# Loading w4 in five pieces of 11, 9, 5, 2 and 1 rows instead of eight

## Chip, cores, metric

One core of one Trainium2 chip. The metric is the device time of one execution in microseconds. Ratios of times come with a 95% interval; "same" means within 2%. Besides the time there is the profile: the span of one execution (about 1.8 us shorter than the time) and the trace of every instruction, DMA packet and semaphore event in it. In the lines shown from it, PE is TensorE, DVE VectorE, ACT ScalarE and SP the sync engine; a "q" behind the name means the engine's instruction sequencer, and L191 is line 191 of the kernel. A load is counted in 16 completion counts, one from each DMA engine; it has arrived with the last of them.

## The reference

One decoded token goes through two branches whose results are added. Branch A is attention over a cache of 65536 keys (32 query heads, 4 key/value heads of width 128). Branch B is a small mixer and a two-layer MLP:

```python
h2 = _gelu(_layernorm(x1, axis=-1) @ w3) @ w4      # w4: 3584 x 1024, bf16
...
return x + _A_ref(xn, A_k_cache, A_v_cache, A_wq, A_wo) + _B_ref(xn, ...)
```

Every weight and the whole cache are read once, 169.87 MB. There is little arithmetic per byte.

## The kernel before

All large operands pass through three buffers of 8 MB, in a fixed order: wq, w3, w1 and w2, then K and V of eight units, wo between the last K and the last V, and w4 at the end. A load is issued when a buffer comes free. All of them go through the sync engine's one DMA queue, so they run in order.

w4 is laid out as 128 partitions x 28 rows; a "row" here is 1024 bf16 elements (2 KB) in each partition, 256 KB in all. It is loaded in pieces, so that its matmuls can start before all of it is there:

```python
W4_PIECES = (6, 5, 6, 4, 3, 2, 1, 1)
...
            elif it == "w4":
                w4_v = B_w4.rearrange("(m c) n -> m c n", c=FC)
                c0 = 0
                for n in W4_PIECES:
                    go(out=t[:, c0 * D:(c0 + n) * D], in_=w4_v[:, c0:c0 + n, :].rearrange("p c n -> p (c n)"))
                    c0 += n
```

At the end, TensorE adds everything into one PSUM bank (`row_acc`), two matmuls for each row of w4. `early` is the number of rows, 11, that come before the last group's projection:

```python
    add_projection()
    compute_v(NU - 1)
    early = sum(W4_PIECES[:2])
    compute_w4(0, early)
    project(HKV - 1)
    compute_w4(early, FC)

    out_t = ogpool.tile([64, 512], BF16, name="out_t", tag="og")
    nc.scalar.copy(out=out_t[:], in_=psB[0:64, :])
    nc.scalar.dma_start(out=out[0, 0, :].rearrange("(j n) -> j n", j=2), ...)
```

One thing is not in this source. The framework gives each DMA one of eight completion semaphores, in rotation, and at the end it makes the sync engine wait for all of them.

## Time and profile before

| | before |
|---|---|
| time, median of 4 runs | 402.25 us (402.11 to 402.31) |
| span of the profiled run | 400.3 us |
| DMA engines busy | 98.6% of the span (main queue) |
| last V arrives | 379.32 us |
| last of w4 arrives | 396.73 us |
| from there to the end | 3.60 us |

The page's head and some of its lines. The digits are tenths of busy time in 40 equal slices of the span; the line "q1" gives packets, MB and busy share of the sync engine's queue.

```profile
span 400.3 us, 2563 instructions
PE 236.0 (59%) x1348; PEld 45.2 (11%) x854; DVE 208.9 (52%) x154; ACT 27.3 (7%) x35; POOL 5.3 (1%) x28
...
DMA  9998999999999999999999999999999998999895
...
q1 hardware_dynamic: 4560, 169.87, 98.6%
```

No compute engine is near full, and the DMA engines are busy nearly everywhere. I read the kernel as bound by its loads.

The chain of waits, its last pieces (start in us, length, what):

```profile
379.33 17.39 DMA big<-in_B_w_dram
396.73 0.04 issue
396.77 0.40 PE psB L191 x2
397.17 0.02 issue
397.19 0.58 ACT out_t L455
```

From the arrival of the last V, w4 streams alone for 17.4 us. After its last byte come two matmuls, the cast and the store.

TensorE in the same stretch (start, length, line, what, count; in brackets its idle time before and what ended it):

```profile
386.21 2.30 PE L191 MATMUL psB<-big,hT 128*1 128x512 bf16 x10
388.44 0.80 PE L403 MATMUL pm_e<-ol,sel8big 128*128 128x129 f32 x2
389.17 1.50 PE L191 MATMUL psB<-big,hT 128*1 128x512 bf16 x12
390.51 1.89 PE L191 MATMUL psB<-big,oT 128*1 128x512 bf16 x16
392.23 2.97 PE L191 MATMUL psB<-big,hT 128*1 128x512 bf16 x26
395.47 1.03 PE L191 MATMUL psB<-big,hT 128*1 128x512 bf16 x6 [0.27 <-DMA big<-in_B_w_dram]
396.77 0.38 PE L191 MATMUL psB<-big,hT 128*1 128x512 bf16 x2 [0.27 <-DMA big<-in_B_w_dram]
```

The matmuls over `hT` are w4's, those over `oT` the last projection. TensorE catches up with the stream and twice waits for it, 0.27 us each. The last two matmuls start 0.04 us after the last arrival.

The sync engine's waits, the lines about w4's issue (L153) and the program's end (L482): total us, times, longest.

```profile
SPq L482 <- DMA big<-in_B_w_dram: 17.0, 3, 15.8
...
SPq L153 <- DMA big<-in_A_v_cache_dram: 14.5, 1, 14.5
...
SPq L482 <- DMA out_dram<-out_t: 2.7, 1, 2.7
```

The last two pieces reuse semaphores of wo and of the last V, and so the last piece could not be issued before the last V had landed. (A further line, 0.6 us for `PEq`, is the meeting of the engines at the very end; it is left out here.)

### The profile page before, as it was taken

The numbers are of one execution on the slowest core, as the hardware profiler recorded it, in microseconds if no ns is written. First come the engines' busy times: TensorE is split into PE (matmuls) and PEld (weight loads), VectorE is DVE, ScalarE is ACT, GpSimd is POOL, SyncE is SP. The second block draws the span as 40 slices with busy tenths as digits, with TensorE's granted clock in tenths as the row PEclk, the third lists the DMA queues.
The fourth block names the chain that finished last, engine by engine and source line by source line (L and its number), as shares of the span: only waits on it lengthen the run. The fifth ranks groups of instructions, "written<-read, shape, count | busy, mean of one in ns | idle before, by whom it ended". The sixth has DMA issues, their size and how long they took to land.

```text
span 400.3 us, 2563 instructions
## 1 busy us (share of the span) xinstructions
PE 236.0 (59%) x1348; PEld 45.2 (11%) x854; DVE 208.9 (52%) x154; ACT 27.3 (7%) x35; POOL 5.3 (1%) x28
## 2 busy tenths in 40 slices
PE   0561960591678247922965195629453946594986
PEld 0210000010200110011102010201020102000222
DVE  1601010965196549644953994279349931975040
ACT  1001010003000200020002000100100020002000
POOL 2000000000000000000000000000000000000000
PEclk9995795597669666978796789568865986697989
DMA  9998999999999999999999999999999998999895
GB/s 419 419 453 371 435 471 458 426 419 419 421 426 465 452 426 414 426 426 432 445 460 426 419 426 419 447 439 452 426 421 426 432 445 385 432 481 426 385 417 201
DMA packets 4575, 170.01 MB, mean 425 GB/s; under 512 B 467, under 2 KB 469, under 8 KB 982
## 3 DMA queue, kind: packets, MB, share of 16 engines
q1 hardware_dynamic: 4560, 169.87, 98.6%
q8 instruction: 8, 0.13, 0.1%
q14 instruction: 1, 0.01, 0.0%
q10 hardware_dynamic: 6, 0.00, 0.0%
HBM read 169.87 MB, written 0.00 MB: 424 GB/s over the span
## 4 chain that ended last, share of the span: by engine, by line
DMA 51%; DVE 26%; PE 16%; ACT 3%; another core or an unknown queue 2%; issue 1%; DVEq 0%; ACTq 0%
DMA big<-in_A_k_cache_dram 31%; DVE big L327 19%; DMA big<-in_A_v_cache_dram 10%; PE sc L332 8%; PE oacc L382 6%; DMA big<-in_A_wq_dram 6%; DMA big<-in_B_w_dram 4%; DVE p_sb L353 3%; DVE mx L337 3%; ACT p_sb L350 3%; PE psq L257 2%; DVE m L341 0%; PE pm_mx L339 0%; PE pm_mx L346 0%
## 5 line engine op out<-in xcount | busy, mean ns | idle before, releaser
L332 PE MATMUL sc<-big,qdiag 128*128 128x512 bf16 x512 | 129.5, 414 | 62.7 <-DVE big L327 57.2
L327 DVE STREAM_TRANSPOSE big<-big 128x4096 f32<-128x4096 f32 x32 | 139.4, 4413 | 49.4 <-DMA big<-in_A_k_cache_dram 49.4
L382 PE MATMUL oacc<-big,p_sb 128*32 128x512 bf16 x512 | 46.9, 539 | 34.5 <-DVE p_sb L353 34.5
L337 DVE TENSOR_REDUCE mx<-sc 128x1 f32<-128x2048 f32 x8 | 18.3, 2291 | 30.0 <-PE sc L332 30.0
L332 PEld LDWEIGHTS <-qdiag 128*128 128x128 bf16 x128 | 13.2, 103 | 174.7 <-issue 145.9
L350 ACT ACTIVATE p_sb<-sc,nball 128x2048 bf16<-128x2048 f32 x8 | 15.7, 1967 | 217.8 <-DVE nball L348 217.8
L353 DVE STREAM_TRANSPOSE p_sb<-p_sb 128x2048 bf16<-128x2048 bf16 x8 | 18.5, 2311 | 18.0 <-ACT p_sb L350 18.0
L382 PEld LDWEIGHTS <-p_sb 128*32 128x32 bf16 x512 | 17.1, 129 | 61.0 <-DVE p_sb L353 35.1
L257 PE MATMUL psh<-big,ln_rep_b 128*32 128x512 bf16 (+1 forms) x64 | 12.4, 941 | 7.6 <-DMA big<-in_B_w_dram 7.6
L421 PE MATMUL o_acc<-big,oT 128*1 128x512 bf16 x48 | 12.8, 437 | 2.4 <-ACT p_sb L350 2.4
L339 PE MATMUL pm_mx<-ident_f,mx 128*1 128x128 f32 x8 | 2.2, 273 | 19.1 <-DVE mx L337 19.1
L296 DVE STREAM_TRANSPOSE h_row<-h_row 128x896 bf16<-128x896 bf16 x1 | 1.1, 1111 | 20.8 <-ACT h_row L295 20.8
L391 DVE SCALAR_TENSOR_TENSOR og<-oacc,wb,og 128x512 f32<-128x512 f32 x4 | 3.0, 746 | 16.7 <-PE oacc L382 16.7
L191 PE MATMUL psB<-big,hT 128*1 128x512 bf16 x56 | 8.1, 424 | 0.6 <-DMA big<-in_B_w_dram 0.5
L427 DVE COPY o_rows<-o_acc 1x1024 f32<-1x1024 f32 x1 | 1.2, 1211 | 13.6 <-PE oacc L382 13.6
L205 PE MATMUL pm_ln<-ln_rowsum_a,ones_f 128*128 128x1 f32 x2 | 0.6, 348 | 12.5 <-DVE ln_rowsum_a L203 12.5
L403 PE MATMUL pm_e<-ol,sel8big 128*128 128x129 f32 x8 | 2.8, 446 | 7.9 <-DVE ol L402 7.9
L257 PE MATMUL psq<-big,ln_rep_a 128*32 128x512 bf16 x64 | 6.2, 573 | 1.5 <-DMA big<-in_A_wq_dram 1.5
L281 POOL COPY qdiag<-qx 32x32 bf16<-32x32 bf16 x16 | 3.2, 203 | 279.5 <-PE sc L332 249.6
L196 DVE STREAM_TRANSPOSE x_t<-x_row 32x256 bf16<-32x256 bf16 x4 | 2.5, 616 | 8.1 <-DMA x_row<-in_A_x_dram 8.0
L269 DVE CAST q_row<-psq 128x512 bf16<-128x512 f32 x1 | 0.7, 691 | 8.4 <-PE psq L257 8.4
L346 PE MATMUL pm_mx<-ident_f,rep 1*128 1x1 f32 x8 | 1.8, 223 | 5.0 <-DVE rep L343 5.0
(95 smaller groups left out, 73.2 us busy)
## 6 DMA issues: line engine op xcount, KB each, us to landing
big<-in_A_wo_dram SPq DMA_DIRECT2D x1, 8192.0 KB, 36.0
big<-in_B_w_dram SPq DMA_DIRECT2D x1, 7168.0 KB, 38.3
big<-in_B_w_dram SPq DMA_DIRECT2D x2, 2048.0 KB, 46.3
big<-in_B_w_dram SPq DMA_DIRECT2D x2, 1536.0 KB, 27.3
big<-in_B_w_dram SPq DMA_DIRECT2D x1, 1280.0 KB, 24.1
big<-in_B_w_dram SPq DMA_DIRECT2D x1, 1024.0 KB
big<-in_B_w_dram SPq DMA_DIRECT2D x1, 768.0 KB, 30.7
big<-in_B_w_dram SPq DMA_DIRECT2D x1, 512.0 KB, 31.5
```

The costliest lines, as they stand in the source:

```text
L191: nc.tensor.matmul(psB[32 * j:32 * j + lhsT.shape[1], :], lhsT=lhsT, rhs=rhs, start=start, stop=False, tile_position=(0, 32 * j), skip_gro ...
L257: nc.tensor.matmul(acc[32 * q:32 * q + 32, i, 0:n], lhsT=rep[:, c, :], rhs=cols(c, i, q), start=(c == 0), stop=(c == DC - 1), tile_positio ...
L281: nc.gpsimd.tensor_copy(out=qdiag[at, LEAD:].rearrange("p (x c) -> p x c", x=4)[:, :, 32 * a:32 * a + 8], in_=qx[at, :, 8 * g:8 * g + 8])
L327: nc.vector.transpose(out=words, in_=words)
L332: nc.tensor.matmul(sc[:, e, :], lhsT=qdiag[:, c0:c0 + P], rhs=cols[:, s, e, :, b2, :, r], start=(s == 0 and b2 == 0 and r == 0), stop=(s = ...
L337: nc.vector.reduce_max(out=mx[:], in_=sc[:].rearrange("p e n -> p (e n)"), axis=AX.X)
L350: nc.scalar.activation(out=p_sb[:], in_=sc[:], func=ACTF.Exp, bias=nball[:, b:b + 1], scale=SCALE, accum_out=group["lall"][:, b:b + 1])
L353: nc.vector.transpose(out=flat, in_=flat)
L382: nc.tensor.matmul(oacc[32 * q:32 * (q + 1), :], lhsT=pT[:, e, 32 * t:32 * (t + 1)], rhs=vt[:, :, e, t, :], start=(e == 0 and t < 4), stop ...
L391: nc.vector.scalar_tensor_tensor(out=og[:], in0=oacc[:], scalar=wb[:, 1:2], in1=og[:], op0=ALU.mult, op1=ALU.add)
L403: nc.tensor.matmul(pe[:, 0:DH + 1], lhsT=sel8big[:], rhs=ol[:], start=True, stop=True)
L421: nc.tensor.matmul(tail["rows"][0:1, h2, :], lhsT=oT[g][:, j:j + 1], rhs=wt[:, g, j, 512 * h2:512 * (h2 + 1)], start=(g == 0 and j == 0), ...
```

## The change

The intent: fewer and larger transfers in a stretch bound by the DMA engines, with the last piece still one row, so that little work is left behind the last arrival. The first piece covers the same 11 rows as the first two did.

```diff
-W4_PIECES = (6, 5, 6, 4, 3, 2, 1, 1)
+W4_PIECES = (11, 9, 5, 2, 1)
...
-    early = sum(W4_PIECES[:2])
+    early = W4_PIECES[0]
```

## The prediction

> What bounds the kernel now. In the page's slices the 16 DMA engines are 98 to 99% busy almost from end to end, at about 425 GB/s; 169.87 MB have to be read. TensorE is busy 59% of the span, VectorE 52%. The chain of waits ends plainly: V of the last unit lands at 379.33 us, then "DMA big<-in_B_w_dram" takes 17.39 us to 396.73, then two matmuls of 0.40, a ScalarE cast of 0.58, the store, end at 400.3. So w4 streams alone for 17.4 us, and the rest of the work there hides under it.
>
> What the change does. Same 7.34 MB, same slot, same release (first w4 issue at 361.64, 17.7 us before its bytes move). Eight transfers become five. The last piece stays one row, so what follows the last landing is unchanged. Two waits of the sync engine go: the last two pieces reuse the completion semaphores of wo and of the last V (14.5 us in the wait view; last issue only at 379.3). I count this as worth nothing: that piece was still queued 17 us before it landed.
>
> What a transfer costs. The completion counts in the trace put the last arrival of the eight pieces (6, 5, 6, 4, 3, 2, 1, 1 rows) at 383.02, 386.09, 389.80, 392.29, 394.17, 395.43, 396.08 and 396.73. The steps fit 0.61 us per row plus 0.04 per piece. Three pieces fewer: 0.12 us. A second estimate from packet records: medians of 84 ns for 2048 B, 312 for 8192, 613 for 16384, 2420 for 65536 give about 8.6 ns per packet beside the bytes, and a completion takes 9; 24 data packets and 3 completions fewer per engine make 0.23 us. I take 0.12 to 0.23. The Trainium skill, "DMA: Bandwidth & Descriptors", section "Why small descriptors are slow (HBM only)", names a fixed overhead per packet; the trace agrees, at most 8.6 ns here. The same page, "Anatomy of one DMA", fits a fixed 2.0 us per transfer (on another issue path). Three times that would be 6 us; I reject it: the transfers queue back to back, and windows from 380 to 394 us show the engines 99 to 103% busy across four boundaries between pieces.
>
> Does TensorE lose? The first 11 rows had landed by 386.09, and the w4 matmuls started only at 386.21, after the projection rows; the wait for 11 rows costs 0.1 us at most. After the last group's projection, at 392.2, 18 matmuls of the 9-row piece run to 394.3 (0.114 us each, as the 26 there before). I estimate landings at 386.07, 391.6, 394.65, 395.9 and 396.55. Ten matmuls fit between the third and fourth, four between the fourth and fifth (0.5 to 0.6 us: tight). TensorE should still be waiting for the last row.
>
> On the critical path: all of the 0.12 to 0.23 us, as the w4 stream ends the chain. Predicted 402.1 us, range 401.7 to 402.5 (three runs before spread 0.2). Chances: faster by over 2% 0.005, within 2% 0.99, slower 0.005.
>
> Right if: 4128 packets on the sync queue instead of 4560; last w4 landing 17.15 to 17.3 us after V's; two matmuls behind it, after a short wait; five issues in a few us, no wait for V.
>
> Wrong if: a completion costs the stream more than this; the spread between engines (2.0 us from first to last arrival of a piece) changes; or TensorE, kept waiting by coarser pieces, has matmuls left when the last row lands.

## More of the kernel before

The three waits under L482 are the closing ones: first for w4, and only then, for 2.7 us, for the store.

## The result

402.16 us (402.09 to 402.19, 4 runs) against 402.25 (402.11 to 402.31). The ratio is 0.9998, interval 0.9981 to 1.0015: the same. (A ratio is the mean of one kernel's fast runs over the mean of the other's in the same rounds, so it is not quite the ratio of the medians.) Two later batches of five runs gave 402.14 against 402.05 and 402.12 against 402.14. No gain can be seen in the time.

The page after:

```profile
span 400.4 us, 2560 instructions
PE 229.6 (57%) x1348; PEld 44.3 (11%) x854; DVE 209.0 (52%) x154; ACT 27.3 (7%) x35; POOL 5.4 (1%) x28
...
DMA  9998999999999999999999999999999999999994
...
q1 hardware_dynamic: 4128, 169.87, 98.5%
```

432 packets fewer for the same bytes, as predicted. The chain after, its last pieces:

```profile
363.49 33.11 DMA big<-in_B_w_dram
396.60 0.04 issue
396.65 0.40 PE psB L191 x2
397.05 0.02 issue
397.07 0.58 ACT out_t L455
```

The DMA piece is longer only because nothing now ties the last piece's issue to the last V; the chain goes back to its issue at 363. The last row arrives at 396.604 with the last V at 379.408: the stretch is 17.20 us, where it was 17.41 (396.728 less 379.319). The arrivals of V are taken from the semaphore events of the trace, as are those in the tables below. The stream did gain 0.21 us.

But the span did not get shorter. From the last arrival of w4 to the end it is now 3.80 us, where it was 3.60. TensorE, the cast and the issue of the store follow as before (397.07 + 0.58). The sync engine's waits after, the lines that answer to those above (there is none for L153 on V any more):

```profile
SPq L482 <- DMA out_dram<-out_t: 35.4, 1, 35.4
SPq L482 <- PEq L482: 0.6, 2, 0.4
```

The closing waits now begin with the store. The sync engine stands at that wait for 35.4 us, from just after its last issue at 363.5. All the other closing waits come after it, when their loads have long arrived. The trace shows the last completion count of the store at 399.44 us before and 399.32 after, and the end of the span at 400.33 and 400.40. So 0.89 us pass behind the store before, and 1.09 after. That is where the gain seems to have gone. (The last V came 0.09 us later in this profile. Over the 14 profiles it came between 379.20 and 379.50, with no order that I see. Such scatter is as large as the gain, so the arguments below rest on the stretches of the trace and not on the totals.)

TensorE after:

```profile
386.16 1.24 PE L191 MATMUL psB<-big,hT 128*1 128x512 bf16 x9 [0.73 <-DMA big<-in_B_w_dram]
387.32 0.74 PE L403 MATMUL pm_e<-ol,sel8big 128*128 128x129 f32 x2
388.00 3.06 PE L191 MATMUL psB<-big,hT 128*1 128x512 bf16 x13
390.51 2.27 PE L191 MATMUL psB<-big,oT 128*1 128x512 bf16 x16
392.40 4.62 PE L191 MATMUL psB<-big,hT 128*1 128x512 bf16 x34
```

It waits 0.73 us for the first 11 rows, then works almost without a gap to the end. Still its last two matmuls start 0.04 us after the last row's arrival, as before. The coarser pieces used up slack and cost no time.

### The profile page after: what moved, and what is told of

Its sections match the earlier page's. It is cut to its first block, busy times and chain, and to the rows that moved or that the text cites. A ratio compares the mean times of both kernels' runs of the same rounds, so it can differ in the third digit from the quotient of the medians.

```text
span 400.4 us, 2560 instructions
## 1 busy us (share of the span) xinstructions
PE 229.6 (57%) x1348; PEld 44.3 (11%) x854; DVE 209.0 (52%) x154; ACT 27.3 (7%) x35; POOL 5.4 (1%) x28
## 4 chain that ended last, share of the span: by engine, by line
DMA 56%; DVE 24%; PE 14%; ACT 2%; another core or an unknown queue 2%; issue 1%; SPq 0%; DVEq 0%; ACTq 0%
DMA big<-in_A_k_cache_dram 42%; DVE big L327 19%; DMA big<-in_B_w_dram 8%; PE sc L332 8%; DMA big<-in_A_wq_dram 5%; PE oacc L382 4%; DVE p_sb L353 2%; DVE mx L337 2%; ACT p_sb L350 2%; PE psq L257 1%; SPq L153 0%; PE pm_mx L339 0%; DVE m L341 0%; PE pm_mx L346 0%
## 5 line engine op out<-in xcount | busy, mean ns | idle before, releaser
L382 PE MATMUL oacc<-big,p_sb 128*32 128x512 bf16 x512 | 42.2, 502 | 34.5 <-DVE p_sb L353 34.5
L421 PE MATMUL o_acc<-big,oT 128*1 128x512 bf16 x48 | 11.9, 413 | 2.4 <-ACT p_sb L350 2.4
```

The costliest lines, as they stand in the source:

```text
L382: nc.tensor.matmul(oacc[32 * q:32 * (q + 1), :], lhsT=pT[:, e, 32 * t:32 * (t + 1)], rhs=vt[:, :, e, t, :], start=(e == 0 and t < 4), stop ...
L421: nc.tensor.matmul(tail["rows"][0:1, h2, :], lhsT=oT[g][:, j:j + 1], rhs=wt[:, g, j, 512 * h2:512 * (h2 + 1)], start=(g == 0 and j == 0), ...
```

## The experiments

Theory: w4's stretch is bound by the stream; a piece costs its packets and little else; and the saved 0.21 us was given back in the order of the closing waits. Rivals: a transfer has a large cost of its own; nothing changed but noise; the removed wait for V was part of the effect; TensorE, not the stream, holds the end. Twelve runs were made, all with the right result, each timed in five rounds beside the kernel before (for experiment 7 four times are on record). They came in three batches on three chips: experiments 1 to 4, 5 to 8 and 9 to 12; the kernel before had 402.05, 402.24 and 402.14 us in them. The second batch held no run of the changed kernel, so there its stretches are compared with those of the other batches. "Stretch" is the time from the last V's last arrival to w4's last arrival; "close" is from the store's last completion count to the end of the span.

### 1. The changed kernel once more

No edit.

> The changed kernel once more, as the measure for the other three of this batch. My theory: the w4 stretch (last arrival of the last V to last arrival of w4) is 17.2 us again, 0.2 shorter than with eight pieces (17.4), and the total 0.0 to 0.3 us below the kernel before. Rival 'nothing but noise': the stretch is within 0.05 us of 17.4 in this run. Rival 'given back at the end': the stretch is 17.2, but the time from the last w4 arrival to the end of the span is again longer than before (3.8 us against 3.6).

402.14 us against 402.05 before in this batch. Stretch 17.18, close 1.09. Noise is ruled out as the reading of the trace: in three profiles of the changed kernel the stretch is 17.20, 17.18 and 17.21, and the close 1.09 each time. With eight pieces it is 17.41 and, in experiment 11, 17.39.

TensorE took another course in this profile. It ran at its full granted clock from 386.5 to 390 us (1.00, where the profile above had 0.63) and waited three times for pieces, 1.9 us in all. In the third profile (0.56 there) it waited for none long enough to be listed, and the chain view even follows TensorE back instead of the load. In all three the last two matmuls start 0.04 us after the last row's arrival.

### 2. 28 pieces of one row

```diff
-W4_PIECES = (11, 9, 5, 2, 1)
+W4_PIECES = (1,) * 28
...
-    early = W4_PIECES[0]
+    early = 11
```

> 28 pieces of one row, projection still after row 11. Theory: the stretch grows with the pieces. From the fit of arrivals (0.04 us per piece) 23 pieces more than five cost 0.9 us: stretch 18.1 us; from packet records (8.6 ns per packet, 9 per completion: 184 packets and 23 completions more) 1.8 us: stretch 19.0 us. Total 0.7 to 1.6 us above the kernel before. Rival 'a transfer has a large cost of its own, hidden because few were changed': 23 times 0.3 us or more, at least 7 us over. Rival 'the piece count does nothing': under 0.2 us over. The many waits of the sync engine (each issue waits for the piece eight earlier) should cost nothing, since eight pieces in flight are 5 us of stream.

403.93 us, 1.88 over the kernel before, ratio 1.0046 (1.0032 to 1.0059). Stretch 18.74: 1.55 us for 23 more pieces, 0.068 each. This lies in the expected range of the stretch, nearer to the packet estimate. The total is a little over its range. The terms that the range left out are in the trace: the close is 1.08 instead of 0.89, and the last two matmuls took 0.61 us instead of 0.40. The large cost of a transfer (0.3 us or more) is ruled out, and so is no cost at all.

### 3. Five pieces, but packets of one row

```diff
-  go(out=t[:, c0 * D:(c0 + n) * D], in_=w4_v[:, c0:c0 + n, :].rearrange("p c n -> p (c n)"))
+  go(out=t[:, 0:FC * (D + 8)].rearrange("p (c n) -> p c n", c=FC)[:, c0:c0 + n, 0:D], in_=w4_v[:, c0:c0 + n, :])
...
-  row_acc(j, hT[:, c:c + 1], wt[:, D * c + 512 * j:D * c + 512 * (j + 1)])
+  row_acc(j, hT[:, c:c + 1], wt[:, (D + 8) * c + 512 * j:(D + 8) * c + 512 * (j + 1)])
```

> Five pieces as in the changed kernel, but rows laid 1032 elements apart, so that no packet can be longer than 2048 B: as many data packets as with 28 pieces, 23 completions fewer. If what a piece costs is its packets, this run's stretch equals that of the 28 pieces within 0.25 us (18.1 to 19.0 us). If it is the completion (or the transfer as such), the stretch stays near 17.2 to 17.4 us. Matmuls unchanged.

403.73 us, stretch 18.86, close 1.09. The queue lines of the page, first of the 28 pieces:

```profile
q1 hardware_dynamic: 7440, 169.87, 98.6%
```

and of this run:

```profile
q1 hardware_dynamic: 7072, 169.87, 98.7%
```

The difference of 368 packets is 23 completions on 16 engines; the data packets are the same 3584 of 2048 B. With five completions the stretch is as long as with 28 (even 0.12 us longer, which stays unexplained: the padded rows also start at other addresses). So what a piece costs is its packets: (18.86 - 17.18) us over 184 more packets per engine is 9.1 ns per packet, and from 28 pieces, completions included, it is 8.4. The edit changed one thing more: issuing the five pieces took the sync engine 26.9 us, to 388.8. The last issue was still over 9 us ahead of its landing and the DMA engines were full (share 1.04 to 1.05 from 380 to 394 us), so the issue did not hold the stream there.

### 4. Four more rows to read

```diff
                 c0 = 0
+                go(out=t[:, FC * D:(FC + 4) * D], in_=w4_v[:, 0:4, :].rearrange("p c n -> p (c n)"))
                 for n in W4_PIECES:
```

> The changed kernel with four more rows (1 MB) read into unused space ahead of w4. Theory, the w4 stream alone sets the end: 4 x 0.61 + 0.04 = 2.5 us later, total 2.2 to 2.6 us over the changed kernel of this batch. Rival 'the tail is held by TensorE or by the sync engine's waits as much as by the stream': under 1.5 us.

404.39 us, 2.25 over the changed kernel of the batch, as expected; stretch 19.68, 2.50 longer. The stream sets the end almost one for one (the close, 1.02, is 0.07 shorter here, and the last V came 0.27 earlier).

### 5. The last three pieces merged

```diff
-W4_PIECES = (11, 9, 5, 2, 1)
+W4_PIECES = (11, 9, 8)
```

> Pieces 11, 9, 8: the last three of the change merged. Theory: the stream saves 0.1 to 0.15 us, but 16 instead of 2 matmuls stand behind the last arrival; at 0.11 us each (full rate as after the projection) to 0.21 (the slower rate seen at 388 us of the changed kernel) the end comes 1.4 to 2.9 us later than in the changed kernel. Rival 'pieces at the end cost as much as they hide': within 0.3 us of it.

403.37 us, 1.13 over the kernel before in this batch (402.24), ratio 1.0029 (1.0016 to 1.0041). The stretch is 17.08, 0.1 shorter, and the span 1.3 us longer than the changed kernel's. That is just under the expected range. The last pieces of its chain:

```profile
396.49 0.04 issue
396.53 1.91 PE psB L191 x16
398.44 0.02 issue
398.46 0.58 ACT out_t L455
```

16 matmuls took 1.91 us, where two took 0.40. Of these 1.51 us, 0.1 came back in the stream and 0.09 in the close, which is 1.00 here. A short last piece is worth far more than the packets it costs.

### 6. One piece

```diff
-W4_PIECES = (11, 9, 5, 2, 1)
+W4_PIECES = (28,)
...
-    early = W4_PIECES[0]
+    early = 11
```

> w4 in one piece of 28 rows. Theory: last arrival about 0.2 to 0.3 us sooner than with five pieces, then the 56 w4 matmuls and the last projection (16) behind it: 72 x 0.11 to 0.21 us minus the two that stand there anyhow: 7 to 12 us over the changed kernel. Rival 'each transfer costs 2 us as its fixed share': four transfers fewer give 8 us back and the total is about even with the changed kernel.

411.04 us, 8.8 over the kernel before, ratio 1.0228 (1.0214 to 1.0242): slower. The stretch is the shortest of all, 16.92, but 72 matmuls then stand behind it:

```profile
396.37 0.04 issue
396.41 9.67 PE psB L191 x72
```

Four transfers fewer gave 0.26 us back, not 8.

### 7. The first two pieces merged

```diff
-W4_PIECES = (11, 9, 5, 2, 1)
+W4_PIECES = (20, 5, 2, 1)
...
-    early = W4_PIECES[0]
+    early = 11
```

> Pieces 20, 5, 2, 1, projection still after row 11: merges the first two of the change, to see how much slack TensorE has at the front. Theory: its w4 work starts at 391.6 instead of 386.1 us. 40 matmuls of w4, 16 of the projection and the row sums before it (0.8 us) then take at least 6.9 us at 0.114 each, to 398.5, and 16 more for the last three pieces, to 400.3, where the changed kernel is done at 397.0: 2.5 to 4 us over the changed kernel, with the last row long landed. Rival 'TensorE has slack for any first piece': within 0.3 us.

406.74 us, 4.5 over the kernel before, ratio 1.0113 (1.0099 to 1.0127). The last row arrived at 396.49, and nobody waited for it:

```profile
361.67 29.82 DMA big<-in_B_w_dram
391.49 0.04 issue
391.53 10.09 PE psB L191 x72
401.63 0.02 issue
401.65 0.58 ACT out_t L455
```

The direction held, the size was over the range (2.5 to 4 over the changed kernel). I had reckoned with 0.114 us per matmul. The 72 took 0.140 on average. The stretches of the profile, with the granted TensorE clock (PEclk) as third figure from the end:

```profile
391.50:396.00 4.50, 4.47 (x22) 1.40 (x23) 0.00 (x0) 0.00 (x0) 0.00 (x0) 0.51 0.75 305
396.00:402.00 6.00, 5.61 (x52) 2.08 (x48) 0.00 (x0) 0.35 (x1) 0.00 (x0) 1.00 0.00 0
```

In the first stretch, at 0.51, 22 matmuls ran in 4.5 us; in the second, at 1.00, the other 50 in 5.6. So the slack at the front ends somewhere between 11 and 20 rows, and 11 is what the change chose.

### 8. The wait for V put back

```diff
                 for n in W4_PIECES:
+                    if c0 == FC - 1:
+                        for e in range(3):
+                            go(out=t[0:16, FC * D + 512 * e:FC * D + 512 * (e + 1)], in_=w4_v[0:16, 0, 0:512])
```

> The changed kernel with three tiny loads (16 rows of 1 KB) into unused space ahead of the last piece, so that the last piece again reuses the completion semaphore of the last V and is issued only when V has landed (as before the change). Theory: the wait costs nothing; the three small loads add 3 x about 0.05 us to the stream: 0 to 0.3 us over the changed kernel. Rival 'the wait that went was part of the gain, or would cost if the piece got there late': 0.5 us or more over.

402.09 us against 402.24 before in this batch; the changed kernel had 402.14 and 402.12 in the others. The wait is back (the edit moved the lines to L156 and L485), and costs nothing that can be seen in the time:

```profile
SPq L485 <- DMA big<-in_B_w_dram: 17.0, 3, 16.7
SPq L156 <- DMA big<-in_A_v_cache_dram: 14.5, 1, 14.5
SPq L485 <- DMA out_dram<-out_t: 2.7, 1, 2.7
```

There was a second effect, though. The stretch is 17.47, 0.26 to 0.29 longer than in the three profiles of the changed kernel, and still the span is 400.4, that of the changed kernel. Of this, 0.16 lies between the arrivals of the two-row piece and of the last row (0.80 us instead of 0.64), where the tiny loads are; the rest lies before them. The run does not part the wait from the loads. The close is 0.89 instead of 1.09. The three loads had also turned the rotation of the semaphores by three places, to where the kernel before had them.

### What the runs so far say together

The built programs, and the instruction records of the traces, show the closing waits of the sync engine. They are the same in every version, five instructions one after the other (the semaphores are numbered by the rotation, 0 to 7):

```
1  wait DMA semaphores 3 and 2
2  wait DMA semaphores 4 and 1
3  wait DMA semaphores 5 and 0
4  wait DMA semaphore 6 and VectorE
5  wait DMA semaphore 7 and ScalarE
```

The store takes the semaphore that comes next in the rotation after w4's pieces. So the number of pieces decides at which of the five waits the sync engine is held by the store, and how many it must still get through after that. The trace of the changed kernel has them one by one: the first starts at 399.334, 0.02 us after the store's last count, the others at 399.403, 399.470, 399.534 and 399.596. Each takes 27 or 28 ns, and the next starts 62 to 69 ns after it did. In the kernel before, the first three were over by 396.8; the fourth starts at 399.455 and the fifth at 399.517. From the instruction behind the fifth to the end of the span it is 0.743 us in both.

| kernel | pieces | stretch, us | store's semaphore | at wait | close, us |
|---|---|---|---|---|---|
| before | 8 | 17.41 | 6 | 4 | 0.89 |
| changed (experiment 1) | 5 | 17.18 | 3 | 1 | 1.09 |
| 28 pieces | 28 | 18.74 | 2 | 1 | 1.08 |
| packets of one row | 5 | 18.86 | 3 | 1 | 1.09 |
| four more rows | 5 + 1 | 19.68 | 4 | 2 | 1.02 |
| last three merged | 3 | 17.08 | 1 | 2 | 1.00 |
| one piece | 1 | 16.92 | 7 | 5 | 0.82 |
| first two merged | 4 | 17.12 | 2 | 1 | 1.07 |
| wait put back | 5 + 3 tiny | 17.47 | 6 | 4 | 0.89 |

Where only the pieces differ, the stretch falls by 0.067 us per piece from 28 to 1 ((18.74 - 16.92) / 27). The close goes with the place of the wait, and with nothing else in the table. So far the semaphore had moved only together with the loads of w4 or beside them, so the last batch moved it and left w4 alone.

### 9. The changed kernel, same batch

> The changed kernel, as the measure of this batch. w4 stretch 17.2 to 17.3 us (before: 17.4); last arrival of the store's completion to the end of the span 1.08 us (before: 0.885); total within 0.15 us of the kernel before.

402.12 us against 402.14. Stretch 17.21, close 1.09: all as expected.

### 10. The changed kernel with the rotation turned by four

```diff
     nc.scalar.dma_start(out=x_row[0:1, :], in_=A_x[0, 0:1, :])
+    turn = const.tile([1, 64 * 4], BF16, name="turn")
+    for e in range(4):
+        nc.scalar.dma_start(out=turn[:, 64 * e:64 * (e + 1)], in_=A_x[0, 0:1, 64 * e:64 * (e + 1)])
```

> The changed kernel with four tiny loads (128 B each) on the ScalarE queue at the start. They only turn the rotation of the eight completion semaphores by four, so that the store's falls into the last of the sync engine's five closing waits instead of the first. Theory, the stream's gain was given back there: last arrival to end 0.83 us instead of 1.08, total 0.2 to 0.3 us below the changed kernel of this batch and 0.2 to 0.5 below the kernel before. Rival, the longer end has another cause (fewer transfers, chance): 1.08 us again and no change of the total.

401.96 us (401.78 to 402.12). Stretch 17.19, close 0.82, span 399.97 against 400.32. The close came out as expected to 0.01 us; the time is 0.16 under the changed kernel and 0.18 under the kernel before, slightly less than the ranges said. (The profiled run is the fastest of the five; the median of their spans is 400.1.) The closing waits in its profile (the edit moved them to L485):

```profile
SPq L485 <- DMA big<-in_B_w_dram: 32.5, 4, 27.7
SPq L485 <- DMA out_dram<-out_t: 2.7, 1, 2.7
```

The store is waited for last.

### 11. The kernel before with the same turn

The same edit on the kernel before.

> The kernel before (eight pieces) with the same four tiny loads. There they move the store's semaphore from the fourth of the closing waits to the first. Theory: last arrival to end 1.06 to 1.09 us instead of 0.885, total 0.1 to 0.25 us ABOVE the kernel before, and 0.35 to 0.5 above the run with five pieces and the same loads (stream 0.2, end 0.25). Rival, the tiny loads gain or cost something by themselves: both kernels move the same way.

402.28 us (402.23 to 402.32), 0.14 over the kernel before. Stretch 17.39, close 1.06, span 400.53. Its closing waits:

```profile
SPq L485 <- DMA out_dram<-out_t: 19.8, 1, 19.8
SPq L485 <- PEq L485: 0.6, 2, 0.4
```

The same edit shortens the close of one kernel (1.09 to 0.82) and lengthens that of the other (0.89 to 1.06), as the theory asked and the rival could not; the medians moved the same ways (0.16 down, 0.14 up), though by themselves neither is clear of the noise. With the same four loads in both, five pieces beat eight by 0.32 us in the medians, and their five times each do not overlap (401.78 to 402.12, 402.23 to 402.32). The profiled spans differ by 0.56, but they are the fastest run of the one and the slowest of the other; stretch and close make 0.43 of it. The medians give less than the 0.35 to 0.5 expected.

### 12. The changed kernel with the rotation turned by two

The edit of experiment 10 with two loads.

> The changed kernel with two tiny loads: the store's semaphore falls into the third of the five closing waits, a place that no run had yet. So far the first gave 1.06 to 1.09 us, the second 1.00 to 1.02, the fourth 0.88, the fifth 0.83. Theory, about 0.06 us for each wait that follows: 0.92 to 0.97 us, total 0.1 to 0.2 below the changed kernel of this batch.

Close 0.95, span 400.13: the third place fits between its neighbours. The time shows nothing of it: 402.11 us, with one run of 402.42 among the five, against 402.12. Differences of 0.1 us are at the edge of what five runs of this kernel tell apart.

Turned by four, the five pieces have the lowest median of all (experiment 10), 0.18 us of 402 under the kernel before. The ratio, 0.9997, has an interval from 0.9983 to 1.001, and experiment 8 had the same ratio in its batch. It is a demonstration, not a gain to speak of.

## Why the prediction was right

- **The time.** 402.1 was predicted, 402.16 measured, inside 401.7 to 402.5. That proves little: the kernel before, at 402.25, lies in this range too, and no gain was measured. The hit owes something to luck: an effect that was not foreseen took the gain back, and it was too small to leave the range. The step from the stream's gain to the total was wrong all the same, as below.
- **The stream.** "0.12 to 0.23 us" for three pieces fewer: measured 0.21. Of the two estimates, the one from the packet records (24 packets of 8.6 ns, three completions of 9, 0.23 us) was nearer. The fit of the arrivals, 0.04 us per piece, was too low; pieces cost 0.067 over the whole range. The Trainium skill, "DMA: Bandwidth & Descriptors", "Why small descriptors are slow (HBM only)", has a fixed overhead per packet; experiments 2 and 3 show 8.4 and 9.1 ns.
- **The 2 us of a transfer.** Rejected in the prediction, and by experiment 6: four transfers fewer shortened the stretch by 0.26 us. The page's section "Anatomy of one DMA" fits a fixed cost to each DMA on the GpSimd path. In the full queue here nothing of that size adds up, and behind the last data packet of w4 the last count came 0.44 us later (396.16 to 396.60).
- **TensorE.** "Should still be waiting for the last row": it was, by the measure that counts, since the last two matmuls started 0.04 us after the arrival in all three profiles of the changed kernel. "0.1 us at most" for the first 11 rows was too low as a wait (0.73 us, because TensorE was earlier there than before), but it cost nothing. The slack has an end: experiment 7 used it up at the front, with 20 rows, and experiment 5 left too much work for the back.
- **The wait for V.** "Worth nothing": experiment 8 agrees, as far as it parts the wait from the three tiny loads.
- **The step that failed:** "what follows the last landing is unchanged", and so "on the critical path: all of the 0.12 to 0.23 us". From the last arrival to the end it took 3.80 us instead of 3.60. The number of pieces moved the store's semaphore from the fourth of five closing waits to the first, and each wait behind it costs about 0.066 us ((1.087 - 0.824) / 4, from experiments 9 and 10). Three more of them are 0.20 us, which takes back nearly all of the 0.21. Experiments 10 to 12 show this by moving the semaphore alone. Had I followed the rotation to the store, as I did to the last piece, I could have seen that the wait would move; even the cost stands in the trace of the kernel before, where the fifth wait starts 0.062 us after the fourth.

What stays open: why a closing wait that is already satisfied costs 0.066 us, and why the padded rows of experiment 3 took 0.12 us more than the 28 pieces.

## What to carry to other kernels

In the full queue of this kernel a piece cost only its packets, 0.067 us, while the matmuls left behind the last arrival cost their full time (1.51 us for 14 more in experiment 5). Where a trace looks like this one, choose the last piece for the work behind it and the first for the slack ahead, and don't expect a gain from merging the rest. Follow a change to the end of the program: a different number of DMAs can shift which semaphore the last one gets, and what waits on it. When a gain seen in the trace doesn't appear in the time, compare the stretches one after the other; what took it back may have nothing to do with what was changed.

## What the Trainium skill lacked or had wrong

- "DMA: Bandwidth & Descriptors", "Rules for kernel authors": it asks for at least 1 MiB per DMA for full bandwidth. Here 28 transfers of 256 KB, queued back to back, moved 7.34 MB in 18.74 us, which is 392 GB/s; one transfer of all did it in 16.92 us (434 GB/s). The page could say that in a full queue the price of a piece was 0.067 us.
- The same page, "Measured (HBM→SBUF, 128 partitions, SWDGE, issued from GpSimd)", gives about 10.5 ns per packet on that path, the span of its smallest transfer over 64 packets. That is another quantity. What the page lacks is the price of one more packet at the same bytes: on the sync engine's queue the runs show 8.4 to 9.1 ns.
- No page that I found says what a closing wait costs that is already satisfied when it is reached: about 0.066 us each in these runs. "Advanced Engine Details and Errata", "Network/Comms", has 50 to 100 ns for reading a semaphore's value from a sequencer, which fits, but no run here shows that this is the cause.
